# Spreading two token routings over more steps of the attention and expert stages of a fused kernel

## The chip, the core and the metric

The kernel runs on one core of a Trainium2 chip. The core has TensorE (PE, matmuls), VectorE (DVE), ScalarE (ACT), GpSimd (POOL) and SyncE (SP, which issues DMAs). Each runs its own instructions strictly in the order in which the program lists them, and waits for the others by semaphores. The metric is the time of one execution on the device, in microseconds; lower is better.

## What is computed

Three stages follow one another, all in float32:

- Linear attention over 4 batches, 8 heads, 576 tokens and 64 columns: `phi(x)` projects by `w_phi` to 128 features, subtracts the largest absolute value `m` of the row, and takes `exp` of the result and of its negative. Then `kv = phi(k)^T v`, `z = sum phi(k)`, and the output is `phi(q) kv / (phi(q) z + 1e-6)`.
- A mixture of 8 experts on the 2304 tokens of 512 columns: each token's logits are `x @ w_gate` plus a bias chosen by its modality. The token goes to its best expert alone, `relu(x @ w1[e]) @ w2[e]`, weighed by the softmax probability of that expert.
- A gated product for all tokens: `((x @ w_a) * (x @ w_b)) @ w_out`.

The expert of a token is known only at run time, so each half of the tokens (1152, two batches) needs a *routing*: logits, arg max, the rank of every token within its expert, and from these an index table that says which token sits in which row of which expert tile (608 rows), and a second table back.

## The kernel before

**Attention** runs over eight units (two batches by two heads), in nine rounds `r` (`Attn.round`, L100). A round holds for unit `r` the projections `phi(0)` to `phi(4)` (matmuls `pjp`, then VectorE's reduce L156 and difference L157, then ScalarE's exps), the transposes of the query features (`turn`, PSUM tag `q`, two buffers), the kx products (`kx`, PSUM tag `c`, two buffers, evicted by the copy L214) and half of the numerators (`num`, matmuls L231, then L237, L238 and the scaling L242 on VectorE), and for unit `r - 1` the other half and `store`. `store` also sums the gate's logits into `lgp` on GpSimd (L259, L261). `vg` prepares the gate columns of the next unit; its copy is L199. TensorE's order in these rounds is the program's own (`manual_schedule`). `round` has three places for other work, `aside(0)` behind the first kx products, `aside(1)` behind `store`, `aside(2)` at its end.

**The routing** is class `Route`: a list of steps, each some ten short instructions on tiles of [128, 72] or less. `start` makes constants; `gate` adds the bias (L353 to L369); `score` finds the best expert; `rank` counts by ten small matmuls (`rkp`, L391, L393) and normalises the probability `gt`; `place` and `where` compute each token's column `col` and row `pl` in the table; `bounds` computes `meta`, the tile's expert and offsets; `table` makes one-hot operands (L484, L496; GpSimd for the first routing, VectorE for the second), multiplies them on TensorE (`tbp`, L500) and reads the sums into `idx` (L507, L508); `back` does the same for the way back (`tbq`). The first routing's steps stand in the asides of rounds 4 to 8, the second's in the steps of the expert stage (`side`).

**The expert stage** (`Moe.run`) has four tiles of 608 tokens, two for each routing, in 8 steps each: 4 steps of the first layer (`hp`), 4 of the second (`yp`). The rows are fetched by GpSimd's indirect DMAs (`gather`, L577, five a tile), transposed by TensorE (`mxt`, L589) and split into two parts (L592, L593). Expert and offsets are read from `meta` into registers of SyncE and ScalarE (L553, L554). Beside it the third stage's weights are converted (`conv`; GpSimd's L717, VectorE's L728 to L735).

**What sets the order.** A scheduler simulates the engines and lists each one's instructions by priority, that is by their place in the program, as their operands come ready. `low` moves a step behind 80 places; `late` does that too and lets its instructions on VectorE come only behind the last kx copy (`at.copied`); `issue_after(i)` puts instructions behind `i` on the same engine. This list is fixed when the kernel is built: on the chip a short instruction that stands ahead of a long one is waited for.

The steps of the first routing before: round 4 `{2: start, gate}`, 5 `{0: score, 2: rank, place}`, 6 `{0: where, 2: bounds}`, 7 `{0: table}`, 8 `{0: back}`. Those of the second, by step of the expert stage: start 0, gate 0, score 0, rank 2, place 4, where 4, bounds 4, table 8, back 8.

Of the kernel before, what the change touches and what calls it, by code (L numbers as in the profile page):

```python
# [12 lines left out]
BF16 = mybir.dt.bfloat16  # L13
# [45 lines left out]
class Attn:  # L59
# [159 lines left out]
    def num(self, u, *parts):  # L219
# [20 lines left out]
        for b, h in parts:  # L240
            k = 4 if b < 2 else 2
            nc.vector.tensor_mul(x[:, 4 * b:4 * b + 4, h, :] if b < 2 else x[:, 8, :, :], ps[:, o:o + k, 0:72],  # L242
                                 rec[:, o:o + k].unsqueeze(2).to_broadcast([P, k, 72]))
            o += k

    def store(self, u):
# [89 lines left out]
class Route:  # L336
    def __init__(self, tc, pool, lgp, bs, bp):
        self.tc, self.nc = tc, tc.nc
        self.pool, self.lgp, self.bs, self.bp = pool, lgp, bs, bp

    def steps(self, wk, ps, tag, after=None):
# [6 lines left out]
        return [start, self.gate, self.score, self.rank, self.place, self.where, self.bounds, self.table, self.back]  # L348
# [4 lines left out]
    def gate(self):  # L353
        nc, c = self.nc, self.cst
# [6 lines left out]
        nc.vector.tensor_copy(mf, mi)  # L361
        tmp = self.w([NG, E], "bstmp")
        sel = self.w([NG], "bsel")
        for m in range(2):
            nc.vector.tensor_scalar(out=sel, in0=mf, scalar1=float(m), scalar2=None, op0=ALU.is_equal)
            nc.vector.tensor_mul(tmp, sel.unsqueeze(2).to_broadcast([P, NG, E]),
                                 bb[:, m, :].unsqueeze(1).to_broadcast([P, NG, E]))
            nc.vector.tensor_add(lg, lg if m else self.lgp, tmp)
        self.lg = lg  # L369

    def score(self):
# [4 lines left out]
        ex = self.w([NG, E], "bstmp")  # L376
# [10 lines left out]
    def rank(self):  # L387
# [9 lines left out]
        gt = self.gt = self.w([NG], "gt")  # L397
        nc.vector.tensor_reduce(out=gt, in_=self.ex, op=ALU.add, axis=AX.X)
        nc.vector.tensor_scalar_add(gt, gt, 1e-9)
        nc.vector.reciprocal(gt, gt)  # L400

    def place(self):
# [8 lines left out]
        pf = self.w([2, E], "pf")  # L411
        for i in range(2):
            nc.vector.tensor_mul(big, c["m8"], tv[:, i, :].unsqueeze(1).to_broadcast([P, E, E]))
            nc.vector.tensor_reduce(out=pf[:, i, :], in_=big, op=ALU.add, axis=AX.X)
        self.tv, self.pf, self.vals = tv, pf, self.w([3, NG], "vals")
# [33 lines left out]
    def bounds(self):  # L449
        nc, c, tv, pf = self.nc, self.cst, self.tv, self.pf  # L450
# [5 lines left out]
        lo = self.w([NTMAX, E], "lo")  # L456
        hi = self.w([NTMAX, E], "hi")
        te_, of_ = pf[:, 0, :], pf[:, 1, :]
        end = self.w([E], "end")
        nc.vector.tensor_add(end, te_, tv[:, 0, :])  # L460
        it = c["it"].unsqueeze(2).to_broadcast([P, NTMAX, E])
        meta = self.w([3 * NTMAX + 1], "meta")
# [676 lines left out]
```

## Time and profile before

| | us |
|---|---|
| median of 3 runs (814.98 to 819.0) | 816.0 |
| the profiled execution, its own time | 819.03 |
| its span, first to last instruction | 817.2 |
| TensorE busy | 799.0 |
| VectorE busy | 602.8 |
| ScalarE busy | 376.6 |
| GpSimd busy | 136.3 |
| attention and first routing, until the first expert matmul | 0 to 167 |
| expert stage with the second routing | 167 to 392 |
| gated product | 393 to 812 |

Times of rows count from the start of the span. Busy times of engines overlap, so they don't add up; a matmul's end is modelled. Where an engine stood idle, the row of the instruction behind the hole says how long and who released it. "Issue" stands for a hole in which the engine waited for nothing that the profile shows. The granted clock is 1.00 at 2.4 GHz and 0.50 at 1.2 GHz.

### The profile page before, as it was taken

To read this page: it belongs to the slowest core of one execution; us is meant where nothing else is said; L and a number is where in the kernel's file an instruction comes from. 1 tells how busy PE (TensorE), PEld (TensorE's weight loads), DVE (VectorE), ACT (ScalarE), POOL (GpSimd) and SP (SyncE) were. 2 spreads that over 40 slices of the span, in tenths; PEclk is the share of its full clock that TensorE was granted. 3 is DMA by queue.
4 is the path that set the end of the run, shared out by engine and by line. 5 is a ranking of instruction groups with operands and counts; after the bars stand their busy time and mean duration, and the time that the engine had idled before them with its cause. 6 is when DMAs were issued, how large, how long until landed. Compare 5 with 4: busy or idle time off the path is not lost.

```text
span 817.2 us, 18324 instructions
## 1 busy us (share of the span) xinstructions
PE 799.0 (98%) x7283; PEld 752.5 (92%) x7284; DVE 602.8 (74%) x1071; ACT 376.6 (46%) x666; POOL 136.3 (17%) x164
## 2 busy tenths in 40 slices
PE   8999998899999999999999999999999999999996
PEld 7999888799999999999999999999999999999995
DVE  6888899599999999974588897764555585544553
ACT  4556544544445555543445444543333364333333
POOL 2000009532326532200112020030000002000002
PEclk9999999999999999999999999999999999999999
DMA  8765432476579887763789787876566658665642
GB/s 304 215 192 162 154 111 82 131 258 198 209 285 338 330 294 274 255 238 114 271 323 364 261 309 260 272 274 202 185 229 205 198 184 302 207 199 193 214 130 89
DMA packets 85163, 184.22 MB, mean 225 GB/s; under 512 B 27760, under 2 KB 37520, under 8 KB 85072
## 3 DMA queue, kind: packets, MB, share of 16 engines
q1 hardware_dynamic: 81872, 173.21, 62.2%
q0 software_dynamic: 3040, 9.72, 3.4%
q8 instruction: 58, 0.95, 0.5%
q14 instruction: 33, 0.27, 0.1%
q10 hardware_dynamic: 160, 0.07, 0.0%
HBM read 145.21 MB, written 37.75 MB: 224 GB/s over the span
## 4 chain that ended last, share of the span: by engine, by line
issue 46%; POOL 3%; PE 2%; POOLq 0%; ACT 0%; ACTq 0%
POOL out L853 2%; POOL cvs L717 1%; PE abp L54 1%; PE abp L56 1%; PE abp L55 1%; POOLq L1136 0%; PE op L55 0%; PE op L54 0%; PE op L56 0%; ACT cvs L716 0%; POOLq L853 0%; POOLq L717 0%; ACTq L884 0%; ACT pc L897 0%
## 5 line engine op out<-in xcount | busy, mean ns | idle before, releaser
L897 ACT COPY pc<-abp 128x384 f32<-128x384 f32 x252 | 120.9, 480 | 193.7 <-PE abp L56 189.7
L54 PE MATMUL abp<-yh,fw 128*128 128x384 f32 x504 | 170.1, 337 | 1.5 <-ACTq L1062 1.0
L56 PE MATMUL abp<-yh,fw 128*128 128x384 f32 x504 | 170.0, 337 | 0.0
L55 PE MATMUL abp<-yl,fw 128*128 128x384 f32 x504 | 169.8, 337 | 0.0
L54 PEld LDWEIGHTS abp<-yh,fw 128*128 128x128 f32 x504 | 94.6, 188 | 10.6 <-ACT pc L897 1.3
L55 PEld LDWEIGHTS abp<-yl,fw 128*128 128x128 f32 x504 | 94.7, 188 | 7.5
L717 POOL TENSOR_SCALAR cvs<-cvs 128x768 f32<-128x768 f32 x24 | 60.3, 2511 | 218.0 <-ACT cvs L716 217.9
L56 PEld LDWEIGHTS abp<-yh,fw 128*128 128x128 f32 x504 | 94.6, 188 | 0.0
L55 PE MATMUL op<-fw,gh 128*128 128x512 f32 x216 | 85.7, 397 | 0.0
L54 PE MATMUL op<-fw,gh 128*128 128x512 f32 x216 | 85.1, 394 | 0.0
L56 PE MATMUL op<-fw,gl 128*128 128x512 f32 x216 | 85.0, 394 | 0.0
L55 PE MATMUL yp<-hl,wh 128*128 128x304 f32 x256 | 77.4, 303 | 0.8 <-DVE hl L608 0.8
L54 PE MATMUL hp<-mxh,wh 128*128 128x304 f32 x256 | 78.0, 305 | 0.0
L55 PE MATMUL hp<-mxl,wh 128*128 128x304 f32 x256 | 77.8, 304 | 0.0
L56 PE MATMUL hp<-mxh,wl 128*128 128x304 f32 x256 | 77.7, 304 | 0.0
L56 PE MATMUL yp<-hh,wl 128*128 128x304 f32 x256 | 77.6, 304 | 0.0
L54 PE MATMUL yp<-hh,wh 128*128 128x304 f32 x256 | 77.0, 303 | 0.0
L853 POOL DMA_INDIRECT out<-o,perm x18 | 18.4, 1020 | 310.6 <-ACT o L852 303.1
L190 ACT ACTIVATE qts<-qtp 128x512 f32<-128x512 f32 (+1 forms) x80 | 38.3, 557 | 58.3 <-PE qtp L187 50.2
L908 DVE TENSOR_TENSOR d<-u,pc 128x768 f32<-128x768 f32 x36 | 34.4, 957 | 28.8 <-ACT pc L897 28.8
L885 DVE TENSOR_TENSOR gl<-ca,gh 128x384 fp32r<-128x384 f32 x72 | 40.8, 574 | 16.4 <-ACT gh L884 15.4
L156 DVE TENSOR_REDUCE m<-pjp 128x8 f32<-128x1024 f32 (+2 forms) x49 | 45.1, 934 | 9.5 <-PE pjp L154 9.5
(191 smaller groups left out, 1595.7 us busy)
## 6 DMA issues: line engine op xcount, KB each, us to landing
fw<-wsc SPq DMA_DIRECT2D x72, 512.0 KB
fw<-wsc SPq DMA_DIRECT2D x144, 256.0 KB
raw<-in_moe_w SPq DMA_DIRECT2D x24, 768.0 KB
s<-in_moe_w SPq DMA_DIRECT2D x32, 512.0 KB
fw<-wsc SPq DMA_DIRECT2D x72, 128.0 KB
wsc<-whi SPq DMA_DIRECT2D x12, 640.0 KB
wsc<-wsum SPq DMA_DIRECT2D x12, 640.0 KB
wsc<-whi SPq DMA_DIRECT2D x12, 512.0 KB
```

What stands on the lines that cost most here:

```text
L54: nc.tensor.matmul(out, lh, rh, start=start, stop=False)
L55: nc.tensor.matmul(out, lh, rl, start=False, stop=False)
L56: return nc.tensor.matmul(out, ll, rh, start=False, stop=stop).ins
L156: nc.vector.tensor_reduce(out=mv, in_=pv, op=ALU.max, axis=AX.X, apply_absolute_value=True)
L190: nc.scalar.activation(t[:, s, :n, :], ps[:, :n, :], AF.Exp, scale=1.0 - 2.0 * s)
L717: nc.gpsimd.tensor_scalar(out=s.bitcast(F32), in0=s.bitcast(F32), scalar1=LEAST, scalar2=None, op0=ALU.max)
L853: st = nc.gpsimd.indirect_dma_start(out=self.out[:, :], out_offset=bass.IndirectOffsetOnAxis(ap=self.routes[bp].perm[:, c:c + 1], axis=0), ...
L885: self.gl = nc.vector.tensor_sub(gl, ca[:, i, :], f32(gh)).ins
L897: self.copied = copied = nc.scalar.copy(x, ps).ins
L908: nc.vector.tensor_add(d, u, x.unsqueeze(1).to_broadcast([P, 2, n]))
```

## The change

The routing's nine steps become twelve: `spans` (the interval table, with five instructions on GpSimd in the first routing) and `sort` (place and bucket for the way back) come out of `bounds`, and `norm` (the normalised probability in three bfloat16 parts) out of `rank` and `back`. In the first routing, seven instructions of `gate` go to GpSimd (`eng`). The new places: round 4 `{2: start, gate}`, 5 `{0: score, 2: rank, place}`, 6 `{1: where, 2: spans}`, 7 `{0: sort, 1: bounds, table, 2: norm}`, 8 `{0: back}`. `where` and `bounds` come behind the last scaling of `num` (`scaled`), and the table's PSUM comes from tag `q` of the transposes. In the second routing each piece has a step: 0 start and gate, 1 score, 2 rank, 3 place, 4 where, 5 spans and sort, 6 bounds, 8 table, norm and back. In the expert stage, only the first of the first tile's transposes may come ahead of the last kx copy, and the second tile's gathers come behind the last sum of the logits (`ended`).

```diff
-            nc.vector.tensor_mul(x[:, 4 * b:4 * b + 4, h, :] if b < 2 else x[:, 8, :, :], ps[:, o:o + k, 0:72],
+            self.scaled = nc.vector.tensor_mul(x[:, 4 * b:4 * b + 4, h, :] if b < 2 else x[:, 8, :, :], ps[:, o:o + k, 0:72],
...
+            self.ended = added
...
+        self.eng = tc.nc.vector if bp else tc.nc.gpsimd
...
-        return [start, self.gate, self.score, self.rank, self.place, self.where, self.bounds, self.table, self.back]
+        return [start, self.gate, self.score, self.rank, self.place, self.where, self.spans, self.sort, self.bounds, self.table, self.norm, self.back]
...
-        nc.vector.tensor_copy(mf, mi)
+        eng.tensor_copy(mf, mi)
...
-            nc.vector.tensor_scalar(out=sel, in0=mf, scalar1=float(m), scalar2=None, op0=ALU.is_equal)
-            nc.vector.tensor_mul(tmp, sel.unsqueeze(2).to_broadcast([P, NG, E]),
+            eng.tensor_scalar(out=sel, in0=mf, scalar1=float(m), scalar2=None, op0=ALU.is_equal)
+            eng.tensor_mul(tmp, sel.unsqueeze(2).to_broadcast([P, NG, E]),
...
-            nc.vector.tensor_add(lg, lg if m else self.lgp, tmp)
+            eng.tensor_add(lg, lg if m else self.lgp, tmp)
...
-        gt = self.gt = self.w([NG], "gt")
-        nc.vector.tensor_reduce(out=gt, in_=self.ex, op=ALU.add, axis=AX.X)
-        nc.vector.tensor_scalar_add(gt, gt, 1e-9)
-        nc.vector.reciprocal(gt, gt)
...
+    def prefix(self, i):
+        nc, big = self.nc, self.w([E, E], "big")
+        nc.vector.tensor_mul(big, self.cst["m8"], self.tv[:, i, :].unsqueeze(1).to_broadcast([P, E, E]))
+        nc.vector.tensor_reduce(out=self.pf[:, i, :], in_=big, op=ALU.add, axis=AX.X)
+
+    def sort(self):
+        nc, c, pf = self.nc, self.cst, self.pf
         of = self.pick(2, pf[:, 1, :].unsqueeze(1).to_broadcast([P, NG, E]))
         pc = self.w([NG], "pc")
         nc.vector.tensor_add(pc, of, self.vals[:, 0, :])
         self.cq = self.floordiv(pc, c["kp"][:, 1:NG], "cq")
         self.cl = self.over(pc, self.cq, P, "cl")
...
+    def spans(self):
+        nc, c, tv, pf, eng = self.nc, self.cst, self.tv, self.pf, self.eng
+        self.prefix(1)
...
+        eng.tensor_sub(lo, lo, hi)
+        eng.tensor_scalar(out=b2, in0=te_, scalar1=-float(TS), scalar2=None, op0=ALU.mult)
+        eng.tensor_add(b2, b2, of_)
+        eng.tensor_add(span, c["ittS"].unsqueeze(2).to_broadcast([P, NTMAX, E]),
+                       b2.unsqueeze(1).to_broadcast([P, NTMAX, E]))
+        eng.tensor_mul(span, span, lo)
...
-    def table(self):
+    def table(self, ps=None, tag=None):
...
-        hi, lo = self.lookup("tbp", self.col, n, self.pl, self.toks)
+        hi, lo = self.lookup("tbp", self.col, n, self.pl, self.toks, ps, tag)
...
-            with behind(at and at.copied, j > 1), behind(at and at.last, j > 2):
+            with behind(at and at.copied, j > 0), behind(at and at.last, j > 2):
                 self.transp(Ts[0], j)
...
                     for i in range(XG):
-                        self.gather(get(n + 1), i)
+                        with behind(at and at.ended, not n):
+                            self.gather(get(n + 1), i)
...
-def late(tc, step, at):
+def late(tc, step, at, scaled=False):
     def run():
-        with tc.high_priority(offset=-LOWR), tc.issue_after(at.copied):
+        with tc.high_priority(offset=-LOWR), tc.issue_after(at.scaled if scaled else at.copied):
             step()
...
-                rsteps = [low(tc, rsteps[0])] + [late(tc, st, at) for st in rsteps[1:7]] + [low(tc, rsteps[7])]
+                rsteps = [(late(tc, st, at, i in (5, 8)) if i not in (0, 9) else low(tc, st)) for i, st in enumerate(rsteps[:11])]
+                rsteps[9] = low(tc, lambda: routes[0].table(at.ps_q, "q"))
...
-            at.round(r, {4: {2: rsteps[:2]}, 5: {0: rsteps[2:3], 2: rsteps[3:5]}, 6: {0: rsteps[5:6], 2: rsteps[6:7]},
-                         7: {0: rsteps[7:8]}, 8: {0: rsteps[8:]}}.get(r, {}) if r > 2 else {})
+            at.round(r, {4: {2: rsteps[:2]}, 5: {0: rsteps[2:3], 2: rsteps[3:5]}, 6: {1: rsteps[5:6], 2: rsteps[6:7]},
+                         7: {0: rsteps[7:8], 1: rsteps[8:10], 2: rsteps[10:11]}, 8: {0: rsteps[11:]}}.get(r, {}) if r > 2 else {})
...
-        for f, k in enumerate((0, 0, 0, 2, 4, 4, 4, 8, 8)):
+        for f, k in enumerate((0, 0, 1, 2, 3, 4, 5, 5, 6, 8, 8, 8)):
             side.setdefault(k, []).append(low(tc, rs[f]))
```

## Rows read from the trace of the kernel before

**Rows 1.** Part 1 of the page: busy time, share of the span, instructions.

```profile
PE 799.0 (98%) x7283; PEld 752.5 (92%) x7284; DVE 602.8 (74%) x1071; ACT 376.6 (46%) x666; POOL 136.3 (17%) x164
```

**Rows 2.** Windows of 10 us: length, then busy us of each engine (instructions), PEclk, DMA, GB/s.

```profile
130.00:140.00 10.00, 8.69 (x224) 8.20 (x222) 9.69 (x34) 2.25 (x5) 8.60 (x20) 1.00 0.21 50
...
180.00:190.00 10.00, 10.00 (x74) 9.36 (x72) 9.86 (x13) 4.76 (x6) 3.27 (x2) 1.00 0.56 187
```

**Rows 3.** Timeline of TensorE, 92 to 176 us: start, us, operation, [idle time before <-releaser].

```profile
99.02 0.41 PE L211 MATMUL kxp<-v,kp 128*64 128x73 f32 x5 [1.59 <-issue]
...
111.43 2.23 PE L231 MATMUL nmp<-kx,qts 128*64 128x73 f32 x64
...
113.93 0.21 PE L391 MATMUL rkp<-oh,ltri 128*128 128x80 bf16 x1 [0.27 <-DVE x L242]
...
126.82 1.09 PE L187 MATMUL qtp<-ident,df 128*128 128x128 f32 x8 [1.04 <-DVE df L157]
...
133.98 1.24 PE L231 MATMUL nmp<-kx,qts 128*64 128x73 f32 x32 [1.31 <-DVE meta L466]
...
140.40 0.55 PE L500 MATMUL tbp<-tbpr,tbpl 128*128 128x90 bf16 x9
...
143.24 2.83 PE L231 MATMUL nmp<-kx,qts 128*64 128x73 f32 x80
...
155.00 3.59 PE L231 MATMUL nmp<-kx,qts 128*64 128x73 f32 x64 [1.88 <-DVE kx L214]
...
167.10 0.38 PE L54 MATMUL hp<-mxh,wh 128*128 128x304 f32 x1
```

**Rows 4.** Window of half a microsecond at the end of round 7, columns of rows 2.

```profile
155.00:155.50 0.50, 0.50 (x8) 0.50 (x10) 0.43 (x1) 0.50 (x2) 0.50 (x1) 0.50 0.15 57
```

**Rows 5.** Timeline of VectorE, 92 to 176 us.

```profile
111.01 0.22 DVE L398 TENSOR_REDUCE gt<-bstmp 128x9 f32<-128x72 f32 x1
...
112.84 0.18 DVE L523 CAST gp<-grest 128x9 bf16<-128x9 f32 x1
...
117.26 0.22 DVE L431 TENSOR_TENSOR sel<-oh,pf 128x72 f32<-128x72 bf16 x1
...
120.61 0.16 DVE L438 TENSOR_TENSOR jtc<-vals,kts 128x9 f32<-128x9 f32 x1
...
121.83 1.22 DVE L156 TENSOR_REDUCE m<-pjp 128x8 f32<-128x1024 f32 x1
...
131.03 1.30 DVE L431 TENSOR_TENSOR sel<-oh,pf 128x72 f32<-128x72 bf16 x1
...
133.54 0.29 DVE L199 COPY v<-vgp 128x144 f32<-128x144 f32 x1
...
134.83 0.17 DVE L478 CAST meta<-meta 1x28 int32<-1x28 f32 x1
```

**Rows 6.** Timeline of GpSimd, 84 to 176 us.

```profile
121.94 1.21 POOL L484 TENSOR_SCALAR tbpl<-i,pl 128x128 bf16<-128x128 f32 x2 [13.21 <-DVE col L427]
...
130.51 1.68 POOL L496 TENSOR_TENSOR tbpr<-tbph,tokp 128x405 bf16<-128x405 bf16 x2
...
134.29 2.69 POOL L484 TENSOR_SCALAR tbqh<-icol,cqq 128x9 bf16<-128x9 f32 x9 [1.32 <-DVE cqq L441]
...
142.68 0.90 POOL L496 TENSOR_TENSOR tbqr<-tbqh,gp 128x81 bf16<-128x81 bf16 x3
...
143.73 1.11 POOL L577 DMA_INDIRECT xg<-xs,idx  x1
```

**Rows 7.** Groups by form: out<-in xcount | busy us, mean ns of one.

```profile
L259 POOL TENSOR_TENSOR lgp<-lgp,x 128x72 f32<-128x72 f32 x6 | 2.1, 344 | 12.1 <-DVE x L242 12.0
...
L368 DVE TENSOR_TENSOR lg<-lgp,bstmp 128x72 f32<-128x72 f32 x2 | 0.5, 232 | 0.1
```

**Rows 8.** Timeline of TensorE, 201.5 to 203.7 us, behind the second routing's first steps.

```profile
203.30 0.41 PE L55 MATMUL yp<-hl,wh 128*128 128x304 f32 x1 [0.84 <-DVE hl L608]
```

**Rows 9.** Instructions that read tile meta: duration min/median/max in ns, first and last start.

```profile
L554 ACTq TENSOR_LOAD <-meta x8: 278/294/663, 135.0 to 227.5; - x8
```

More of the change, by code (lines that the diff above doesn't have):

```diff
@@ L410, in place @@
         nc.vector.tensor_reduce(out=tv[:, 0, :], in_=big[:, :, :KMAX], op=ALU.add, axis=AX.X)
[L411 to L415, printed above, removed]
+        self.tv, self.pf, self.vals = tv, self.w([2, E], "pf"), self.w([3, NG], "vals")
+        self.prefix(0)
+        pf = self.pf
         self.pick(0, R[:, :NG, :])
@@ L455, in bounds @@
         self.cl = self.over(pc, self.cq, P, "cl")
-        lo = self.w([NTMAX, E], "lo")
-        hi = self.w([NTMAX, E], "hi")
+    def spans(self):
+        nc, c, tv, pf, eng = self.nc, self.cst, self.tv, self.pf, self.eng
+        self.prefix(1)
         te_, of_ = pf[:, 0, :], pf[:, 1, :]
-        end = self.w([E], "end")
+        lo, hi, span = (self.w([NTMAX, E], n) for n in ("lo", "hi", "span"))
+        end, b2 = self.w([E], "end"), self.w([E], "b2")
+        it = c["it"].unsqueeze(2).to_broadcast([P, NTMAX, E])
@@ L467, in bounds @@
-        nc.vector.tensor_sub(lo, lo, hi)
-        b2 = self.w([E], "b2")
-        nc.vector.scalar_tensor_tensor(out=b2, in0=te_, scalar=-float(TS), in1=of_, op0=ALU.mult, op1=ALU.add)
-        nc.vector.tensor_add(hi, c["ittS"].unsqueeze(2).to_broadcast([P, NTMAX, E]),
-                             b2.unsqueeze(1).to_broadcast([P, NTMAX, E]))
-        nc.vector.tensor_mul(hi, hi, lo)
-        nc.vector.tensor_reduce(out=meta[:, NTMAX:2 * NTMAX], in_=hi, op=ALU.add, axis=AX.X)
+        eng.tensor_sub(lo, lo, hi)
@@ new lines, in spans, with bounds @@
+        eng.tensor_scalar(out=b2, in0=te_, scalar1=-float(TS), scalar2=None, op0=ALU.mult)
[3 more added lines that the diff above has]
+        eng.tensor_mul(span, span, lo)
+        self.hi, self.span, self.end = hi, span, end
+    def bounds(self):
+        nc = self.nc
+        meta = self.w([3 * NTMAX + 1], "meta")
+        nc.vector.tensor_reduce(out=meta[:, :NTMAX], in_=self.hi, op=ALU.add, axis=AX.X)
+        nc.vector.tensor_scalar(out=meta[:, :NTMAX], in0=meta[:, :NTMAX], scalar1=float(E - 1), scalar2=None, op0=ALU.min)
+        nc.vector.tensor_reduce(out=meta[:, NTMAX:2 * NTMAX], in_=self.span, op=ALU.add, axis=AX.X)
@@ L474, in bounds @@
         nc.vector.tensor_scalar(out=meta[:, 2 * NTMAX:3 * NTMAX], in0=meta[:, NTMAX:2 * NTMAX], scalar1=float(CG),
                                 scalar2=float(HALF), op0=ALU.add, op1=ALU.min)
-        nc.vector.tensor_copy(meta[:, 3 * NTMAX:], end[:, E - 1:E])
+        nc.vector.tensor_copy(meta[:, 3 * NTMAX:], self.end[:, E - 1:E])
         self.meta = self.pool.tile([1, 3 * NTMAX + 1], I32, name=f"meta{self.bp}")
@@ L513, in table, with norm @@
         self.idx = self.pool.tile([P, n], I32, name=f"idx{self.bp}")
-        hi, lo = self.lookup("tbp", self.col, n, self.pl, self.toks)
+        hi, lo = self.lookup("tbp", self.col, n, self.pl, self.toks, ps, tag)
         self.token(self.idx, hi, lo, 0)
-    def back(self, ps=None, tag=None):
+    def norm(self):
         nc = self.nc
-        gp = self.w([3, NG], "gp", BF16)
+        gt = self.gt = self.w([NG], "gt")
+        nc.vector.tensor_reduce(out=gt, in_=self.ex, op=ALU.add, axis=AX.X)
+        nc.vector.tensor_scalar_add(gt, gt, 1e-9)
+        nc.vector.reciprocal(gt, gt)
+        gp = self.gp = self.w([3, NG], "gp", BF16)
         rest = self.w([NG], "grest")
@@ L525, in back @@
                 nc.vector.tensor_sub(rest, rest, gp[:, i, :])
+    def back(self, ps=None, tag=None):
+        nc, gp = self.nc, self.gp
         self.g2 = self.pool.tile([P, NG], F32, name=f"g2{self.bp}")
```

11 lines of the change are left out of this document (3 added, 8 removed).

## The prediction, made before the changed kernel was run

> **What bounds the kernel now.** I read the page's busy times first, then windows, then TensorE's waits one by one, then what VectorE and GpSimd did under each. TensorE is busy for 98% of the span [rows 1], so only its holes can be won. Those that the change can reach lie beside the first routing, between 110 and 167 us, and one small one behind the second. VectorE is the reason for most: from 130 to 140 us it is idle for 0.31 us in all [rows 2].
>
> The holes of TensorE [rows 3]: 1.59 us at 99.02, in the middle of the kx products, put down to "issue" (no engine is late; I take it to stay); 0.27 us ahead of the rank's matmul; 1.04 us ahead of round 6's transposes, waiting for `df`; 1.31 us ahead of the second half of `num`; and 1.88 us at 155.00, the end of round 7, waiting for the `kx` copy. Behind the last one the granted clock is 0.50, the 1.2 GHz level [rows 4], and the 64 matmuls there last 3.59 us where the same 64 last 2.23 us at 111.43 [rows 3]: 1.36 us more. Without the first these are 0.27 + 1.04 + 1.31 + 1.88 + 1.36 = 5.86 us, and 0.84 us stand behind the second routing [rows 8]: 6.7 us, 0.8% of the span, is all that can be won.
>
> **The change, part by part.**
>
> *Round 5: the gate's normalisation leaves.* Ten VectorE instructions, from the reduce at 111.01 to the cast at 112.84, stand ahead of the `x` product that frees the rank's PSUM [rows 5]. They are 1.9 us of queue; they go to the end of round 7, where VectorE waits for TensorE anyway (that wait is their cover; if it goes, they still come behind the `kx` copy, and `back` needs them only in round 8). Gain 0.27, bounds 0 and 0.27.
>
> *Round 6: `where` moves behind the scaled `x`.* Its eight instructions hold VectorE from 120.61 to 121.83, and the projection's reduce comes behind them [rows 5]. These 1.22 us of queue became 1.04 us of hole, so there is 0.2 us of slack at this point. Without `where` some backlog of `place` stays, which itself loses two instructions. Gain 0.9, bounds 0 and 1.04.
>
> *Round 6's end: `bounds` shrinks.* Some twenty instructions, 131.03 to 135.00, stand around the `v` copy at 133.54, whose PSUM the second `num` needs [rows 5]. Afterwards the slot holds `where` (eight) and VectorE's five of `spans`; five others go to GpSimd. One of the old ones lasted 1.30 us, where the same kind at 117.26 takes 0.22, beside GpSimd's two `tbpr` products of 1.68 us at 130.51 [rows 5, 6]; these products now run later. The Trainium skill, SBUF — State Buffer, section Who interferes with whom, says that a VectorE instruction with two SBUF inputs and a GpSimd instruction that reads SBUF exclude each other for the whole instruction; the 1.30 us agree with that. Gain 1.0, bounds -0.5 (thirteen instructions in two chains in the slot) and 1.31.
>
> *The gate on GpSimd.* Seven instructions; a 72-wide add is 0.34 us there and 0.23 us on VectorE [rows 7]. TensorE lost nothing to the gate, and GpSimd idles at that time, so 0. If GpSimd were late, the score in round 5 would wait, over 5 us later.
>
> *Round 7: `sort` in the place that `where` had.* Six instructions of the kinds of `where`, some 1.2 us ahead of the same reduce. That costs between 0 and 1.04 us by round 6; but the table's matmuls (0.55 us at 140.40 [rows 3], moved from ahead of this stretch into it) now lie between and cover half. Cost 0.2.
>
> *The table waits for GpSimd.* In the old order `where` ends at 121.8 and the table's operands take GpSimd from 121.94 to 132.19, 10.2 us [rows 6]; the matmul came at 140.4, so nobody waited. Now `where` ends near 131.0 (its slot at 131.03, less the 1.2 us won before it, plus 1.2). GpSimd then has five of `spans` (some 1.5 us by rows 7) and 10.2 us: ready near 142.7. TensorE reaches the table behind `num` of round 7, which began at 143.24 and took 2.83 us [rows 3], less 2.2 us won and 0.55 us for the table that stood ahead: 143.3. A cover of 8 us has shrunk to half a microsecond. Cost 0.3, bounds 0 and 2.5.
>
> *End of round 7.* One transpose group instead of two stands between the kx products and `num`; the indices come later, so the gathers (143.73 on [rows 6]) move out of this stretch to about 150. What must stay is the `kx` copy's latency, some 0.7 us (an estimate: a copy of 292 columns, between the 72-wide and the 1,024-wide ones of rows 5, and two hand-overs). The records don't say why the copy came so late, so the gain is anything from 0 to 1.88 + 1.36 = 3.2 us; I take 1.9, a little over half, which is the clock's part and the hole less the copy.
>
> *Gathers and back's operands share GpSimd.* 23 instructions for `back`, 134.29 to 143.58 or 9.3 us [rows 6], ran ahead of the gathers. Now they start when the table's are done, near 143, and the indices come near 146 to 149. If all of `back` goes first, the fifth gather, at 1.1 us each, ends near 158, and the first tile's last transposes wait 1 to 2 us for its landing; if the gathers go first, `back`'s matmul in round 8 waits up to 3 us. Cost 0.5, bounds 0 and 3. The next tile's gathers behind `ended` cost nothing: their transposes come four steps, over 25 us, later.
>
> *The second routing* has the same work, one piece a step. Ten instructions of the norm leave the first two steps, where VectorE is 99% busy [rows 2]; TensorE's 0.84 us at 203.30 wait for VectorE [rows 8]. Against that, `bounds` is two steps later, and ScalarE's reads of its table [rows 9] stand in its queue ahead of evictions. Gain 0.4, bounds 0.84 and -1.
>
> **The sum:** -0.27 - 0.9 - 1.0 + 0.2 + 0.3 - 1.9 + 0.5 - 0.4 = -3.5 us. Behind 167.10, the first expert matmul [rows 3], TensorE has almost no holes, so all of it reaches the end. The profiled execution took 819.03 us (span 817.2), 3.0 above the median 816.0: against itself 815.5, against the median **812.5 us**. A measurement of this kernel tells about 0.5%, 4.1 us, from no change: faster means below 811.9, slower above 820.1.
>
> **The rivals.**
>
> *The end of round 7 clears wholly* (810.0): 3.2 in place of 1.9, no late gather, no late table, the whole 0.84: -0.27 - 0.9 - 1.0 + 0.2 - 3.2 - 0.8 = -6.0. For it: the gathers and the second transpose group, all that was special in that stretch, leave it. Against it: they only move on by some 7 us.
>
> *The moved pieces cost again where they land* (about 816.5). `sort` now stands beside the table's long row of GpSimd instructions. By the one row of 1.30 us, two-input instructions can be held there: four of the six, each by up to one GpSimd instruction of 0.6 us (two took 1.21 us at 121.94 [rows 6]), 2.4 us, of which the table's 0.55 are covered: 1.9 in place of 0.2. With round 7's end as it was and no gain behind: -0.27 - 0.9 - 1.0 + 1.9 + 0.3 + 0.5 = +0.5. That the change doesn't do what it says, because the scheduler, which orders VectorE by its own timeline, puts the low pieces back into the same slots, ends here too. Against it: VectorE's short cast at 134.83 kept 0.17 us beside GpSimd's comparisons from 134.29 [rows 5, 6].
>
> *Slower: the table's PSUM* (820.4). The table now takes one of the two buffers that the transposes rotate through. The second transpose group of round 7 needs it back, and gets it when VectorE has read the table: two short instructions of low priority. If these come behind the reduce and the difference of the last projection, 1.22 us each by rows 5, themselves behind the `x` products that end near 146.1, TensorE stands from about 145.4 to 149.1, 3.7 us, with the clock's 1.4 us behind it as in rows 4. Then nothing is won at round 7's end, the table's own wait is 1.0 and the gathers come 0.5 later: -0.27 - 0.9 - 1.0 + 3.7 + 1.4 + 1.0 + 0.5 = +4.4. It decides from where the two reads come later than the first transposes' end. Against it: the table is done a microsecond before that projection, so a scheduler has a slot for them.
>
> **How the numbers follow.** Forecast 0.40 (a third of it below 811.9, 0.6 us away), clearing wholly 0.26, costing again 0.21, slower 0.13. Faster: 0.26 + 0.14 = 0.40; same: 0.26 + 0.21 = 0.47; slower: 0.13. The range leaves out most of the slow case and the far end of the best: 808.0 to 818.5.
>
> **What would show it.** In the changed profile: no hole ahead of the rank or of round 6's transposes; less than 0.4 us ahead of `num` in round 6; the table's matmul right behind `num` of round 7; the first expert matmul near 164. Wrong would be a hole over 1 us at the second transposes of round 7, the granted clock at half again, or a first expert matmul later than 166.

## The result and the profile after

The changed kernel took **823.89 us** (median of 4 runs, 821.97 to 824.83), the kernel before 816.45 in the same set (4 runs): a ratio of 1.0087, interval 1.0066 to 1.0108 (the ratios given here are not quotients of the two medians and differ from these by up to 0.0014). It is slower by 7.4 us where 3.5 us less were forecast, and it lies outside the range. The two profiled executions are closer to each other than the medians: the one of before is its slowest run (819.03), the one of after its fastest (821.97, span 820.2). So the kernel before was profiled once more, as the first experiment: 814.17 us, span 812.4. That execution has neither the hole at the end of round 7 nor the half clock behind it [rows 3, 4], and it is what after is compared with here. It is the fastest of its twelve runs, as the profiled execution of after is the fastest of its four.

TensorE in the changed kernel's timeline, the places of [rows 3, 8]:

```profile
114.24 0.21 PE L393 MATMUL rkp<-oh,ltri 128*128 128x80 bf16 x1
...
126.06 1.09 PE L187 MATMUL qtp<-ident,df 128*128 128x128 f32 x8
...
131.36 2.25 PE L231 MATMUL nmp<-kx,qts 128*64 128x73 f32 x64 [0.51 <-DVE big L447]
...
141.14 2.76 PE L231 MATMUL nmp<-kx,qts 128*64 128x73 f32 x80
143.84 0.55 PE L508 MATMUL tbp<-tbpr,tbpl 128*128 128x90 bf16 x9
144.79 1.16 PE L154 MATMUL pjp<-wp,qk 64*128 64x128 f32 x16 [0.41 <-DVE df L157]
147.18 0.63 PE L187 MATMUL qtp<-ident,df 128*128 128x128 f32 x4 [1.23 <-DVE rec L238]
149.20 1.09 PE L187 MATMUL qtp<-ident,df 128*128 128x128 f32 x4 [1.39 <-DVE meta L480]
...
156.89 0.66 PE L604 MATMUL mxt<-ident,xg 128*128 128x128 f32 x4 [3.00 <-DMA xg<-xs,idx]
157.47 2.25 PE L231 MATMUL nmp<-kx,qts 128*64 128x73 f32 x64
...
168.53 0.55 PE L604 MATMUL mxt<-ident,xg 96*128 96x96 f32 x4 [0.53 <-DVE mxl L608]
168.87 0.39 PE L54 MATMUL hp<-mxh,wh 128*128 128x304 f32 x1
...
184.27 0.38 PE L54 MATMUL hp<-mxh,wh 128*128 128x304 f32 x1 [1.11 <-DVE hl L623]
```

The same engine in the second trace of the kernel before:

```profile
144.24 2.76 PE L231 MATMUL nmp<-kx,qts 128*64 128x73 f32 x80
...
153.19 2.25 PE L231 MATMUL nmp<-kx,qts 128*64 128x73 f32 x64
...
163.61 0.38 PE L54 MATMUL hp<-mxh,wh 128*128 128x304 f32 x1
```

Up to round 7 the change does what it was forecast to do. The rank's matmul and round 6's transposes have no bracket any more, and the 1.31 us ahead of `num` have become 0.51. Round 7's first `num` starts 3.10 us earlier than in the second trace of before (0.55 of it is the table, which now comes later, and 0.47 stands already at round 5's `num`, which starts at 111.97 here and at 112.44 there). Then it turns: the next `num` starts 4.28 us later. Between the two lie 0.41, 1.23, 1.39 and 3.00 us of holes, 6.03 in all, and a stretch at the 1.2 GHz level. Windows of the changed kernel, columns as in [rows 2], the granted clock third from the end:

```profile
149.00:152.00 3.00, 2.80 (x34) 2.50 (x36) 2.73 (x6) 1.08 (x2) 2.83 (x7) 0.50 0.43 99
...
168.00:190.00 22.00, 19.94 (x142) 19.47 (x142) 20.93 (x53) 9.50 (x14) 10.05 (x10) 1.00 0.82 277
```

and of the second trace of before, the same stretches of the program:

```profile
150.00:155.00 5.00, 5.00 (x136) 4.75 (x132) 4.28 (x7) 2.35 (x5) 3.81 (x6) 1.00 0.66 159
...
163.00:184.00 21.00, 21.00 (x151) 20.67 (x151) 19.35 (x58) 9.77 (x14) 9.04 (x7) 1.00 0.87 294
```

Three microseconds at half clock make TensorE some 1.4 us later there. That isn't a price at the end, because the 3.00 us of waiting for the gather follow and cover it. A later trace of the same code up to here (experiment 11) has the half clock until 155 and waits 1.47 us, and the transposes stand 44.9 us behind round 5's `num` in both (111.82 to 156.68 and 111.97 to 156.89):

```profile
149.00:155.00 6.00, 5.94 (x84) 5.63 (x84) 2.61 (x5) 1.09 (x2) 5.30 (x9) 0.50 0.62 162
```

```profile
156.68 0.65 PE L604 MATMUL mxt<-ident,xg 128*128 128x128 f32 x4 [1.47 <-DMA xg<-xs,idx]
```

The first expert matmul comes 5.26 us later (163.61 to 168.87). TensorE idles for 2.06 of the 22 us from 168, of which 0.53 stand ahead of that matmul, and not at all in the 21 us from 163 in before. VectorE of the changed kernel shows why, first in round 7, then in the second routing's first steps:

```profile
139.81 1.81 DVE L454 TENSOR_TENSOR pc<-vals 128x9 f32<-128x9 f32 x1
...
142.10 1.21 DVE L156 TENSOR_REDUCE m<-pjp 128x8 f32<-128x1024 f32 x1
...
148.86 0.19 DVE L516 TENSOR_TENSOR idx<-tk,tbp 128x45 int32<-128x45 f32 x1
...
177.18 2.70 DVE L535 CAST gp<-grest 128x9 bf16<-128x9 f32 x1
...
183.34 0.78 DVE L623 SCALAR_TENSOR_TENSOR hl<-hp,hh 128x608 fp32r<-128x608 f32 x1
```

and GpSimd:

```profile
139.88 1.69 POOL L504 TENSOR_TENSOR tbpr<-tbph,tokp 128x405 bf16<-128x405 bf16 x2
...
144.96 5.22 POOL L492 TENSOR_SCALAR tbql<-i,cl 128x128 bf16<-128x128 f32 x9
...
151.21 1.12 POOL L592 DMA_INDIRECT xg<-xs,idx  x1 [0.17 <-issue]
...
171.54 1.02 POOL L592 DMA_INDIRECT xg<-xs,idx  x1 [0.35 <-issue]
...
177.68 4.28 POOL L733 TENSOR_SCALAR cvs<-cvs 128x768 f32<-128x768 f32 x2
```

Three things are to be seen. An add of `sort` is held for 1.81 us, exactly while GpSimd makes the table's products, and the projection's reduce stands behind it. The indices are ready at 149.05, but the first gather starts at 151.21: the one-hots of `back` stand ahead of it on GpSimd. They did so before, too (142.44 and 144.74 in the second trace); there TensorE came to those rows at 152.16 and didn't wait. And the second tile's gathers, now at 171.54 and behind, push the weights' clamps into one row with them, beside which a 9-wide cast of the norm takes 2.70 us; `hl`, for which TensorE waits at 184.27, is queued behind that cast. These were three suspects; the experiments price them.

### The profile page after: what moved, and what is told of

It reads as the page before. It is cut to its first block, busy times and chain, and to the rows that moved or that the text cites. A ratio compares the mean times of both kernels' runs of the same rounds, so it can differ in the third digit from the quotient of the medians.

```text
span 820.2 us, 18329 instructions
## 1 busy us (share of the span) xinstructions
PE 798.6 (97%) x7284; PEld 751.5 (92%) x7284; DVE 603.5 (74%) x1061; ACT 376.8 (46%) x666; POOL 137.4 (17%) x176
## 4 chain that ended last, share of the span: by engine, by line
PE 34%; issue 16%; ACT 1%; DVE 1%; POOL 1%; POOLq 0%; DVEq 0%
PE abp L54 7%; PE abp L56 7%; PE abp L55 7%; PE op L55 4%; PE op L54 4%; PE op L56 4%; POOL out L869 1%; ACT pc L913 0%; DVE gl L901 0%; DVE ca L899 0%; ACT yh L813 0%; DVE o L866 0%; POOLq L1153 0%; ACT gh L900 0%; DVE ca L929 0%
```

## The experiments

Ratios are to the kernel before on the same chip. On one chip the kernel before took 820.03 us (25 runs) and not 816; the runs marked * lie there, and their ratios are taken against that. The changed kernel itself was not run on that chip, so a gain or a loss against it is less sure for these.

**1. The kernel before again.**

> The kernel before, unchanged, for a second trace of it. Theory 'the traced stall is an outlier': the profiled execution shown of it took 819.03 us, 3 us above its median, and its hole of 1.88 us at the end of round 7 with the half clock behind it (1.36 us) is what those 3 us are; then a profiled execution near 816 shows neither, the granted clock stays above 0.9 from 150 to 160 us and the first expert matmul comes near 164. Rival 'the stall is there in every execution': the hole and the half clock stand again, and the first expert matmul comes near 167. Ratio 1.000 either way, within 0.002.

816.43 us, ratio 1.0004 (0.9992 to 1.0017); the profiled execution took 814.17, shown above. The stall is not there and the first expert matmul comes at 163.61. So the first theory holds as far as one more trace can show it: the 1.88 us and the half clock are not in every execution. This one is the fastest of twelve, not a median one; but the traces of experiments 3 and 12, which keep the old order at this place, don't have the stall either (their 64 `num` products take 2.25 us).

**2 and 3. Which half of the change.** In the one kernel the second routing has its old steps, in the other the first routing its old places:

```diff
-        for f, k in enumerate((0, 0, 1, 2, 3, 4, 5, 5, 6, 8, 8, 8)):
+        for f, k in enumerate((0, 0, 0, 2, 4, 4, 4, 4, 4, 8, 2, 8)):
```

```diff
+            at.round(r, {4: {2: rsteps[:2]}, 5: {0: rsteps[2:3], 2: rsteps[3:5]}, 6: {0: rsteps[5:6], 2: rsteps[6:9]},
+                         7: {0: rsteps[9:10]}, 8: {0: rsteps[10:]}}.get(r, {}) if r > 2 else {})
...
+        self.eng = tc.nc.vector
```

(and the table, the transposes and the gathers as before; `norm` does not return to `rank`, it stands ahead of `back` in round 8).

> The changed kernel with the second routing's pieces back at the steps they had (everything up to spans and bounds at steps 0, 2 and 4, table and back at 8). Theory 'round 7 of the first routing costs it all': no more than the 1.1 us hole behind the second routing goes, 822.5 to 824, ratio 1.008 to 1.010. Theory 'the second routing's spread costs it': back to about 817, ratio 1.001.

> The changed kernel with the first routing's pieces back in the asides they had, on VectorE, the table in its old PSUM and the gathers unheld; the second routing stays spread. Theory 'round 7 of the first routing costs it all': 815.5 to 817, ratio 0.999 to 1.001, first expert matmul where the kernel before has it. Theory 'the second routing's spread costs it': 822 to 824, ratio 1.008 to 1.010.

1.0081 (1.0061 to 1.0101) and 0.9993 (0.9982 to 1.0003). All of the loss hangs on the first routing's part. The second routing's spread alone neither costs nor gains anything that can be measured; with its old steps the hole behind its first pieces stands too (1.10 us), so it is not made by the spread.

**4. The table's PSUM.**

```diff
-                rsteps[9] = low(tc, lambda: routes[0].table(at.ps_q, "q"))
+                rsteps[9] = low(tc, routes[0].table)
```

> The changed kernel with the table's matmul alone back in the PSUM buffers of the vg, kx and num products. Theory 'the table's PSUM is the main cost': the 1.39 us hole ahead of the second transposes of round 7 goes, and with it the half clock behind it (about 1.5 us): 820.5 to 821.5, ratio 1.0055 to 1.007. Rival 'the late gather sets the end': TensorE reaches the first table rows' transposes earlier and waits there for the same gather, the hole of 3.0 us grows to about 5, time unchanged at 823 to 824.5, ratio 1.008 to 1.010.

1.0091 (1.0071 to 1.0111). The time is the rival's, the mechanism neither's: the wait for the gather shrinks, where the rival let it grow to 5 us. TensorE's timeline:

```profile
147.52 0.83 PE L508 MATMUL tbp<-tbpr,tbpl 128*128 128x90 bf16 x9 [3.84 <-DVE rec L237]
...
156.39 0.65 PE L604 MATMUL mxt<-ident,xg 128*128 128x128 f32 x4 [1.14 <-DMA xg<-xs,idx]
```

With the table in the other buffers, it waits itself, until VectorE has scaled the `x` of the `num` ahead of it. Either buffer comes free only through VectorE's queue; which one it is only says where the same lateness shows. From round 7's first `num` to the first gathered rows it is 15.5 us here (140.92 to 156.39) and 15.75 in the changed kernel, and the time is the same.

**5*. The 32 `num` products ahead of the first table rows' transposes.**

```diff
-            with behind(at and at.copied, j > 0), behind(at and at.last, j > 2):
+            with behind(at and at.copied, j > 0), behind(at and at.half, True), behind(at and at.last, j > 2):
```

(`at.half` is the last product of that `num`.)

> The changed kernel, only TensorE's order differs: the first table rows' transposes come behind the 32 num products at the end of round 7 in place of ahead of them. Theory 'TensorE idles 3.0 us at 153.89 for the first gather': the 32 products fill most of it, hole at most 0.7 us, first expert matmul 2.0 to 2.8 us earlier than 168.9, time 821 to 822, ratio 1.0060 to 1.0075. Rival 'the row of gathers sets the end': the wait comes back ahead of the later transposes, first expert matmul as before, 823 to 824.5, ratio 1.008 to 1.010.

1.0045 (1.0025 to 1.0064), a lower ratio than the theory asked for; the twelve runs spread from 821.3 to 827.3 us. The trace doesn't bear the theory out. The wait for the gather is gone from that place, but 2.47 us put to "issue" stand there instead, the 64 products behind them take 3.93 us, at half clock, and the first expert matmul comes at 168.90, no earlier than in the changed kernel, which was the rival's sign. How the ratio comes about stays open.

**6*. `sort` back in round 6.**

```diff
-... 6: {1: rsteps[5:6], 2: rsteps[6:7]}, 7: {0: rsteps[7:8], 1: rsteps[8:10], ...
+... 6: {1: rsteps[5:6], 2: rsteps[6:8]}, 7: {0: rsteps[:0], 1: rsteps[8:10], ...
```

(`...` marks what is cut from a line; here and in experiments 7 to 9 and 13, `at.half` with `j > 0` keeps TensorE's order that of the changed kernel).

> The changed kernel with sort back at the end of round 6 (behind spans); where, bounds, norm, the table's PSUM and the gathers stay, and TensorE's order in the attention is the same. Theory 'VectorE is late in round 7 because sort stands there, one of its adds held 1.81 us beside GpSimd': the holes of 1.23 and 1.39 us at 146 to 149 and the half clock behind them (1.7 us) go, round 6's num hole grows from 0.5 to about 1.3 us: 820 to 821.5, ratio 1.005 to 1.007. Rival 'bounds and the table's reads alone keep VectorE late': hole at 148 stays at 1 us or more with the half clock, 823 to 824.5, ratio 1.008 to 1.010.

1.0080 (1.0061 to 1.0100), the rival's ratio, with one hole of 4.93 us in place of the two. TensorE, VectorE and GpSimd:

```profile
150.29 1.09 PE L187 MATMUL qtp<-ident,df 128*128 128x128 f32 x4 [4.93 <-DVE meta L480]
```

```profile
149.74 0.23 DVE L481 TENSOR_REDUCE meta<-span 128x9 f32<-128x72 f32 x1 [3.79 <-POOL span L473]
...
149.95 0.19 DVE L516 TENSOR_TENSOR idx<-tk,tbp 128x45 int32<-128x45 f32 x1
```

```profile
144.18 4.67 POOL L492 TENSOR_SCALAR tbql<-i,cl 128x128 bf16<-128x128 f32 x8
...
149.35 0.36 POOL L473 TENSOR_TENSOR span<-span,lo 128x72 f32<-128x72 f32 x1
```

An early `sort` makes `back`'s one-hots ready early; they come ahead of the last product of `spans` on GpSimd; a reduce of `bounds` on VectorE waits for that product; the read of the table is queued behind the reduce; and the table's buffer is what TensorE's transposes wait for. Neither theory had this chain; it comes of splitting `spans` over two engines that both keep their order. The ratio isn't the chain's price alone: behind the hole the trace has another 2.7 us of holes put to "issue" between 154 and 159, and the 64 products take 3.82 us.

**7. `where` back ahead of round 6's projections** (with the changed kernel again beside it):

```diff
-... late(tc, st, at, i in (5, 8)) ...
+... late(tc, st, at, i == 8) ...
...
-... 6: {1: rsteps[5:6], ...
+... 6: {0: rsteps[5:6], ...
```

> The changed kernel, unchanged, beside the three below and for a second trace of it. Theory 'the loss is built in (VectorE late at 142 to 149, gather late at 154), not an accident of one execution': ratio 1.006 to 1.010, the holes of 1.2, 1.4 and about 3.0 us again within 0.1 us, the half clock behind the first two. Rival 'the stretch goes differently in every execution': the sum of these holes differs by over 1 us from 5.6.

> The changed kernel with where alone back ahead of round 6's projections; sort, table, bounds, norm and gathers stay where the change put them. GpSimd has the table's operands done by 133, so nothing of it lies beside sort. Theory 'sort is held by GpSimd's 1.69 us products': the add takes 0.2 in place of 1.81 us, VectorE is 1.6 us earlier in round 7, the two holes at 146 to 149 shrink by 1.2 to 1.6 us, the gathers come 1.6 us or more earlier; round 6's turn hole (1.0) returns: ratio 0.002 to 0.004 below the changed kernel's. Rival 'the table's place behind num makes the loss, whatever where does': holes at 146 to 149 as they were, ratio within 0.001 of the changed kernel's.

The changed kernel: 1.0083 (1.0068 to 1.0098), its holes 1.23, 1.39 and 3.15 us. With `where` early: 1.0088 (1.0075 to 1.0101). The rows of that kernel on VectorE, GpSimd and TensorE:

```profile
140.46 0.17 DVE L454 TENSOR_TENSOR pc<-vals 128x9 f32<-128x9 f32 x1
```

```profile
150.19 1.12 POOL L592 DMA_INDIRECT xg<-xs,idx  x1 [0.17 <-issue]
```

```profile
148.18 0.63 PE L187 MATMUL qtp<-ident,df 128*128 128x128 f32 x4 [1.39 <-DVE meta L480]
...
155.39 0.66 PE L604 MATMUL mxt<-ident,xg 128*128 128x128 f32 x4 [3.90 <-DMA xg<-xs,idx]
155.97 3.88 PE L231 MATMUL nmp<-kx,qts 128*64 128x73 f32 x64
```

The held add is free (0.17 in place of 1.81) and the hole of 1.23 is gone, as the theory had it, yet nothing is won. TensorE arrives earlier and waits 3.90 us for the gather, so the gather sets when the first rows are transposed; its start in turn is set by the 23 instructions of `back` on GpSimd, which begin when `sort` is done. Those transposes do come 1.1 us earlier (43.8 us behind round 5's `num`, which starts at 111.58 here, against 44.9). But the 64 products behind them take 3.88 us, at half clock, where the changed kernel's take 2.25, and the first expert matmul ends up 0.5 us later (57.4 against 56.9). In this execution the clock took back what the earlier gather gave, and the experiment doesn't say what that is worth alone.

**8 and 9. `sort` at the end of round 7; the gathers first.** In the one kernel `sort` leaves VectorE's full stretch, and by that `back`'s operands fall behind the gathers; in the other `sort` stays, and two 9-wide copies at the end of round 7 hold `back`'s operands alone:

```diff
-... 7: {0: rsteps[7:8], 1: rsteps[8:10], 2: rsteps[10:11]}, 8: {0: rsteps[11:]} ...
+... 7: {1: rsteps[8:10], 2: rsteps[7:8] + rsteps[10:11]}, 8: {1: rsteps[11:]} ...
```

```diff
+    def again(self):
+        for n in ("cq", "cl"):
+            t = self.w([NG], n + "2")
+            self.nc.vector.tensor_copy(t, getattr(self, n))
+            setattr(self, n, t)
...
-... 2: rsteps[10:11]}, 8: {0: rsteps[11:]} ...
+... 2: [late(tc, routes[0].again, at)] + rsteps[10:11]}, 8: {1: rsteps[11:]} ...
```

> The changed kernel with sort at the end of round 7 (where VectorE waits for TensorE) and back one aside later; where, table, bounds and gathers' holds stay. The six instructions of sort leave VectorE's queue ahead of the round 7 projections (2.9 us with the held add), and GpSimd's one-hots for back come behind the gathers. Theory 'VectorE's queue in round 7 and GpSimd's order set the loss': the holes at 146 to 149 fall from 2.6 to under 1 us without half clock, the first gather starts within 1 us of its indices and its hole falls from 3.0 to under 2: ratio 0.004 to 0.007 below the changed kernel's. Rival 'late where sets it': the table's matmul or the gather still waits as long, ratio within 0.002 of the changed kernel's.

> The changed kernel with sort where it is, but GpSimd's 23 one-hots and products for back behind the five gathers (two 9-wide copies at the end of round 7 hold them; back's matmul one aside later). Theory 'the first gather waits 2.2 us behind those one-hots': it starts within 1 us of the indices, its hole falls from 3.0 to 1.0 to 1.8 us with the holes at 146 to 149 as they were: ratio 1.0055 to 1.0072. Rival 'sort on VectorE was the cost that the kernel with sort at the end lost': ratio 1.0078 or more.

1.0042 (1.0026 to 1.0058) and 1.0057 (1.0041 to 1.0073). TensorE in the second of them:

```profile
148.56 0.63 PE L187 MATMUL qtp<-ident,df 128*128 128x128 f32 x4 [1.23 <-DVE rec L238]
150.58 0.63 PE L187 MATMUL qtp<-ident,df 128*128 128x128 f32 x4 [1.39 <-DVE meta L482]
...
155.58 0.66 PE L610 MATMUL mxt<-ident,xg 128*128 128x128 f32 x4 [1.69 <-DMA xg<-xs,idx]
...
161.21 0.41 PE L610 MATMUL mxt<-ident,xg 128*128 128x128 f32 x2 [1.05 <-DMA xg<-xs,idx]
```

Both theories hold, the first just (its hole at the second transposes is 1.04 us, where under 1 was asked). GpSimd's order alone gives 0.0026 to 0.0030 back (2.1 to 2.4 us), with VectorE's two holes untouched; `sort` out of VectorE's stretch gives up to 0.0015 (1.2 us) more, for which the intervals are too wide to call it shown. Part of the gather's wait is passed on: 1.05 us now stand ahead of a later row of transposes. The traces show two more things. Of the 2.7 us by which the first rows come earlier in experiment 9 (13.1 us behind round 7's first `num`, at 142.52, against 15.75), only 1.1 are the gather's earlier start; it also takes 1.6 us less from there to the transposes. And neither kernel has the hole of 1.11 us at 184, although the hold on the second tile's gathers stands in both.

**10*, 11 and 12. The second tile's gathers**, not held in the changed kernel (twice), and held in the kernel of experiment 3:

```diff
-                        with behind(at and at.ended, not n):
+                        with behind(at and at.added, not n):
```

> The changed kernel, only GpSimd's order differs: the second tile's gathers no longer wait for the last lgp add (170.85), so they come ahead of it. Theory 'these gathers push the weights' clamp (177.68 to 181.96) under VectorE's short casts, which then take 2.70 and 1.27 us in place of 0.17, and TensorE loses 1.1 us at 183': the hole goes, 822 to 822.8, ratio 1.007 to 1.008, first expert matmul unchanged. Rival 'the casts would be held anyway, or the gathers block the lgp adds': 823.5 to 825, ratio 1.009 to 1.011.

> The changed kernel with the second tile's gathers not held, a second time: its first run lay on a chip where the kernel before took 820 us, with no run of the changed kernel beside it (ratios of that one elsewhere: 1.0081 to 1.0088). Theory 'the hold costs the 1.1 us at 183': ratio 1.0065 to 1.0075, that hole gone. Rival 'it costs nothing at the end': 1.008 or more.

> The kernel with the first routing in its old places (ratio 0.9993), and only the second tile's gathers held behind the last lgp add. Theory 'the hold alone costs, by the clamp behind the gathers on GpSimd': 1.0005 to 1.0020. Rival 'it needs the late first routing': within 0.0006 of 0.9993.

Not held (`at.added` is an earlier sum of the logits, long done): 1.0051 (1.0034 to 1.0067)* and 1.0054 (1.0041 to 1.0067), with no hole left at 184. Held, in the old order: 1.0032 (1.0017 to 1.0047), where the same kernel without the hold had 0.9993; a hole of 2.62 us appears. Its rows on TensorE, VectorE and GpSimd:

```profile
182.81 0.38 PE L54 MATMUL hp<-mxh,wh 128*128 128x304 f32 x1 [2.62 <-DVE hl L623]
```

```profile
175.35 2.65 DVE L533 COPY grest<-gt 128x9 f32<-128x9 f32 x1
178.04 2.07 DVE L535 CAST gp<-grest 128x9 bf16<-128x9 f32 x1
...
181.89 0.78 DVE L623 SCALAR_TENSOR_TENSOR hl<-hp,hh 128x608 fp32r<-128x608 f32 x1
```

```profile
174.85 0.92 POOL L592 DMA_INDIRECT xg<-xs,idx  x1 [0.30 <-issue]
175.80 4.28 POOL L733 TENSOR_SCALAR cvs<-cvs 128x768 f32<-128x768 f32 x2
```

In experiment 1's trace the same two instructions, with a clamp at 170.90 that is long under way:

```profile
172.76 0.37 DVE L521 COPY grest<-gt 128x9 f32<-128x9 f32 x1
173.16 0.18 DVE L523 CAST gp<-grest 128x9 bf16<-128x9 f32 x1
```

So the line that was forecast at nothing costs 0.0029 to 0.0039, 2.4 to 3.2 us; the kernels compared ran on different chips, each against the kernel before there, with intervals of up to 0.0021 either way. The gathers themselves are not late for anything. But held back, they stand ahead of two clamps, which then run without a pause between them, and copies of nine elements wait them out, with the expert's `hl` behind. It is a matter of where the clamps fall: in experiments 8 and 9 the hold stands and TensorE doesn't wait.

**13. Both remedies** (`sort` last, gathers free):

> As the kernel with sort at the end of round 7 (ratio 1.0042), and the second tile's gathers not held. Theory 'the hold costs over 1 us wherever the rest stands, since the gathers push the clamp under VectorE's casts': ratio 1.0025 to 1.0032. Rival: unchanged, 1.004 or more.

1.0046 (1.0033 to 1.0059): the rival. The two gains don't add. The hole at 184 was already gone in experiment 8, so little was left to win there; and the freed gathers now stand ahead of `back`'s operands on GpSimd, which are late already, so that TensorE waits 1.32 us for these ahead of `back`'s matmul.

**14. All three** (`sort` last, `num` ahead, gathers free):

> As the one before, and besides the 32 num products ahead of the first table rows' transposes and the second tile's gathers not held behind the last lgp add. Theory 'the changed kernel loses in three places (VectorE late, gather late, second tile's gathers)': all three are taken out, the gains in rounds 5 and 6 (0.3, 1.0 and 0.8 us) stay: ratio 0.998 to 1.001 against the kernel before. Rival 'what is moved from one place is late in the next': ratio 1.003 or more, a hole of over 1 us ahead of back's matmul or of the last transposes.

1.0068 (1.0054 to 1.0082), again the rival: the profiled execution waits 1.74 us for a gather and 0.87 us ahead of `back`'s matmul, then 2.17 us for the first tile's last pieces. The lateness is handed on.

**15*. A candidate:** the first routing as before, but `spans`, `bounds` and norm at the end of round 7:

```diff
+... 6: {0: rsteps[5:6], 2: [late(tc, routes[0].presort, at), rsteps[7]]},
+... 7: {0: rsteps[9:10], 2: [rsteps[6], rsteps[8], rsteps[10]]}, 8: {0: rsteps[11:]} ...
```

(`presort` is the prefix that `sort` needs.)

> A candidate: the first routing as in the kernel before (where in round 6's aside 0, table in its own PSUM, gathers free, all on VectorE, second routing spread), but spans, bounds and norm leave their tight places for the end of round 7, where VectorE has idle time; sort stays in round 6. Theory 'only what the gathers wait for had to stay early': holes ahead of the rank (0.26) and of round 6's num (1.33, to about 0.4) shrink with nothing new, 814 to 815.2, ratio 0.9975 to 0.9990. Rival 'round 7's end is as tight on VectorE as round 6's': a hole of over 1 us ahead of num at its end with the half clock, 816.5 to 819, ratio 1.0005 to 1.0035.

1.0026 (1.0015 to 1.0036), slower than before, and the rival's ratio. Round 6's holes shrink to 0.57 and 1.00. But at the end of round 7 holes of 0.3 to 0.7 us stand, 1.8 in all, and the 64 `num` products take 3.80 us, at half clock as the rival had it; the first expert matmul comes 4.1 us later than in the second trace of before, counted from round 5's `num` (55.3 us behind 113.04, against 51.2 behind 112.44). Behind that TensorE waits 0.22 and 0.71 us for the first weights and 1.60 for VectorE. VectorE's last instruction of `bounds` and SyncE's issue of the weights, here:

```profile
159.71 0.14 DVE L491 CAST meta<-meta 1x28 int32<-1x28 f32 x1
```

```profile
162.59 7.33 SPq L580 DMA_DIRECT2D s<-in_moe_w  x3
```

and in the second trace of before:

```profile
135.84 0.17 DVE L478 CAST meta<-meta 1x28 int32<-1x28 f32 x1
```

```profile
138.68 0.91 SPq L560 DMA_DIRECT2D s<-in_moe_w  x2
```

Which expert's weights to fetch is read from `meta`, so they can't be issued before `bounds` is done: 2.7 us lie between the two in either kernel. Neither theory asked what else waits for `bounds`. No version here beats both kernels; the best, experiment 3, can't be told from the kernel before.

## Why the prediction was wrong

**Rounds 5 and 6, right.** The norm's 0.27 and `where`'s 1.04 were won whole (0.27 and 0.9 forecast), and of `bounds` 0.8 (1.0 forecast; the 0.51 us that are left miss the sign of less than 0.4). The gate on GpSimd cost nothing that shows.

**The end of round 7, wrong: the step "I take 1.9".** A stall whose cause "the records don't say" was counted as half won. The second trace of before doesn't have it, nor have two other traces of that order (experiment 1), so the median had little or nothing to give. The signs were in the times: the profiled run was the slowest of three, 3.0 us above the median, and hole and half clock made 3.2. The sum went against the profiled run, but then the difference was carried over to the median unchanged, and with it a gain that only that run could give.

**`sort` in round 7, wrong in size:** 0.2 forecast. Against the 0.36 us that the second trace of before has there, 0.41 and 1.23 us of hole stand in its place: 1.3. The rival that says moved pieces cost again had the mechanism, the held two-input add, and 1.9 for it. On that add the Trainium skill, SBUF — State Buffer, section Who interferes with whom, which says that such an instruction contends with one of GpSimd that reads SBUF, agrees with the traces: 1.81 us beside GpSimd's products, 0.17 without them in experiment 7. What the 1.3 us cost at the end is less, since the wait for the gather covers them.

**The table, half right.** It came right behind `num` at 143.84 as forecast, without waiting for GpSimd (0.3 forecast, 0 found). But the rival on its PSUM took place: 1.39 us of hole and some 1.4 of half clock, where the rival had 3.7 and 1.4. Its reason was too narrow: experiment 4 moves the table to the other buffers and the same lateness stands ahead of the table. VectorE is late in this stretch, not the buffer short. And the rival let all of this reach the end, where it lies ahead of the wait for the gather.

**Gathers and `back` on GpSimd, wrong in place and size: "cost 0.5".** The two orders were both worked out, but the wait was put at the first tile's last transposes. It stands at the first ones, ahead of `num`, with 3.00 us (the 0.53 us at the last ones are a wait for VectorE). The 2.2 us that `back`'s one-hots put ahead of the gathers were there before as well; what uncovered them is that the indices come 6.6 us later and TensorE 3 us earlier. GpSimd's order alone is worth 2.1 to 2.4 us (experiment 9).

**"The next tile's gathers behind `ended` cost nothing", wrong:** 2.4 to 3.2 us. That step asked when the gathers' own results are needed (25 us later, which is true) and not what stands behind them on GpSimd. This and the gathers' wait are the largest terms that were missed, and this one needs no late first routing (experiment 12).

**The second routing, -0.4, not found:** its old steps give the same time within the interval. The 0.84 us that were to be won are, like the end of round 7, not in the second trace of before.

Against the second trace of before, the terms from rows are then -2.1 in rounds 5 and 6, +1.3 for `sort`, +1.4 and +1.4 for the table's buffer and the clock, +3.0 for the gather, +0.5 at the last transposes, and +1.5 to +2.1 behind the first expert matmul: +7.0 to +7.6 of the 7.8 us between the two spans. That says where the time stands, not what each cause is worth: a remedy for what lies ahead of the gather only makes its wait longer. Shown by experiments are the first routing's part as a whole (2 and 3), the gathers' place on GpSimd (9) and the hold (10 to 12); what is left of the 7 us without these two, and why the remedies don't add up to all of it, is read from traces alone. Of the signs named ahead, three of the wrong ones came: the hole over 1 us at the second transposes of round 7, the half clock, and a first expert matmul later than 166.

## What to carry to other kernels

A step that is moved or held is to be priced by what is queued behind it on its engine, not only by when its result is needed: five gathers with nothing to hurry for cost 2.4 us or more through two clamps behind them, and experiment 15 moved `bounds` without asking what its table releases. Before a stall is counted as a gain, see that it is in more than one execution; where the profiled run lies 3 us above the median, the stall may be those 3 us. And where several queues are full, a remedy in one place can hand its lateness to the next: of two gains of some 3 us each, the two together gave one.

## What the runs showed of the hardware

Nine-element copies and casts on VectorE take 0.17 to 0.18 us when nothing is in their way; beside gathers and clamps of GpSimd several took longer, the longest 2.70 us in the changed kernel and 2.65 us in experiment 12. In the latter case GpSimd ends a gather at 175.77 and a first clamp (half of 4.28 us from 175.80) near 177.9; the copy begins at 175.35 and ends at 178.00, so it waited through the rest of one and the whole of the other, and the cast behind it (2.07 us) through the second clamp. The Trainium skill, SBUF — State Buffer, section Who interferes with whom, says that a copy or cast can, when its operands allow it, enter a mode that contends for the port pair shared with GpSimd, and that whoever issues first has the pair for the whole instruction while the other blocks. The waits agree with that. That these copies ran in such a mode no trace shows; what the traces add is a wait that goes on past the first of two instructions, as that of `sort`'s add did through both of GpSimd's products.

The half clock doesn't follow from the holes alone. The kernel of experiment 9 has the same two holes as the changed kernel (1.23 and 1.39 us), and its `kx` products behind them run at full speed (0.73 us for sixteen, where after's take 1.24 and 1.00). What decides it stays open. What it costs depends on where it falls: ahead of the wait for the gather nothing (experiment 11's trace), behind it 1.6 us in experiment 7 (3.88 us for the 64 products in place of 2.25) and 1.3 in experiment 2 (3.53).

The first gather took 5.7 us from its start to the transposes that waited for it in the changed kernel (151.21 to 156.89) and 4.1 us in the kernel of experiment 9 (151.46 to 155.58). Why was not tried.
